# First loads in order of need on two queues, a constant zero for the warm-up products, and a new order of the first splits and products

## The chip, the cores and the metric

The kernel runs on one core of a Trainium2 chip. The metric is device time in microseconds (us), taken as the median of several executions. One further execution was recorded by the hardware profiler; every time inside the kernel below comes from that one.

The engines that matter here are PE (TensorE: matrix products into PSUM; its weight loads are shown as PEld), DVE (VectorE), ACT (ScalarE), POOL (GpSimd) and SP (SyncE, which issues most of the transfers). A q behind an engine's name means its sequencer, which issues transfers and handles semaphores.

## The reference

A gated mix of a Fourier mixing layer and a sliding-window attention, on one sequence of 2048 rows of 512 values, all in float32:

```python
x = A_x
g = sigmoid((x * gate_w).sum(-1, keepdims=True))
a = Cr @ (x @ Wr.T) - Ci @ (x @ Wi.T)          # real part of a two-dimensional DFT
q, k, v = split(x @ wqkv)                       # 32 heads of 16, window of 256
b = softmax(mask(q @ k.T / 4)) @ v @ wo
out = g * a + (1 - g) * b
```

## The kernel before

Precision is kept by splitting each float32 operand into a high part (rounded to PE's reduced float32 type, here called F32R) and a low part (what is left). A product of two such operands is three matrix products: high by high, high by low and low by high. The list of these pairs is `TERMS` (line 248); the first number picks the part of the weight `w`, or of `x` in the row projections, the second that of the other operand.

The whole program is one long stream of PE products with an order written by hand (manual schedules for PE, ACT, DVE and SP; POOL's order is left to a planner). The stages run into each other: projections of q, k and v, scores, softmax, attention, the two DFT stages and the output projection. A generator, `dense()` (line 595), yields the dense products, and the attention's work is put between them.

What matters here is how the stream begins, before the stages overlap:

- **Loads** (lines 147 to 159). `wraw` takes the weights of the first group of q and k, 128 x 1024, in four blocks of 256 columns, one for each quarter `dk` of the contraction. `XRAW[dk, 0]` takes the first 512 rows of x, transposed, as four blocks of 128 x 512. ACT's queue issues x blocks 0 and 1; SP's queue issues w block 0, w block 1, x blocks 2 and 3 in one transfer, and w blocks 2 and 3 in one transfer. Behind them SP issues the two halves of the v weights (`wv`, 512 KB each) and the next rows of x.
- **Splits** (lines 160 to 164). For each `dk`: ACT copies w to its high part (`wq0[0]`), x is split by `split_x` (high part by DVE for block 0 and by ACT for blocks 1 to 3, line 80 or 82; low part by DVE, line 85), and then DVE makes w's low part (line 164). Each engine works in this order.
- **Warm-up** (`warm()`, line 590). Eight products of a zero tile (128 x 128 weights, 512 columns, F32R) go to PE before anything else. The zero tile is cleared by DVE at line 151.
- **First products** (`qk_first()`, line 263). 24 products of 512 columns: for each `dk`, for each of the three terms, for q and for k. Each adds into one of two PSUM tiles.
- **What follows.** The v projections (`v_proj` through `row_proj`, line 304) take the same x and the split v weights `wvs` (`late(split_raw, r, True)`, line 601: high parts by ACT, low parts by DVE, behind the splits above on both engines).
- **POOL.** Line 203 fills the unused rows of one pad tile; its input `first_lo` is a piece of `wq0[1]`, read only to give it a place in the order. Eight memsets of the ring's spare rows (line 200) follow.

Tiles come from rotating pools: `pt` has four buffers (the first three hold `wraw` and x's first four blocks), and `ev` has five, one of them the zero tile.

The numbers that a transfer waits for are semaphores. The program has eight of them for transfers and hands them out in program order, so that a ninth transfer waits on its queue until the first has landed.

Of the kernel before, what the change touches and what calls it, by code (L numbers as in the profile page):

```python
# [7 lines left out]
F32 = mybir.dt.float32  # L8
F32R = mybir.dt.float32r
# [5 lines left out]
P = 128  # L15
# [4 lines left out]
NP = 4  # L20
# [6 lines left out]
WARM = 8  # L27
# [5 lines left out]
def fnet_window_mix(ctx: ExitStack, tc: tile.TileContext, xT, x, wqk, wv, wr, wi, cr, ci, wo, gw, out):  # L33
    nc = tc.nc
# [4 lines left out]
    ev = ctx.enter_context(tc.tile_pool(name="ev", bufs=5))  # L39
# [15 lines left out]
    def ld(dst, src):  # L55
        mark("sp", nc.sync.dma_start(dst, src))

    def f(ap):
        return ap.bitcast(F32)
# [4 lines left out]
    def mark(e, ins):  # L64
        last[e] = ins.ins
# [12 lines left out]
    def split(hi, lo, raw, act=False):  # L78
        if act:
            nc.scalar.copy(hi, raw)  # L80
        else:
            cast = (nc.gpsimd if act is None else nc.vector).tensor_copy(hi, raw)
            if act is None:
                mark("pool", cast)
        return nc.vector.tensor_sub(lo, raw, f(hi))
# [44 lines left out]
    XRAW = {}  # L130
# [7 lines left out]
    def split_x(ss, dks, act=False):  # L138
        for dk in dks:
            XT[dk, ss] = big.tile([P, 2, 512], F32R, name="big")  # L140
            mark("dve", split(XT[dk, ss][:, 0], XT[dk, ss][:, 1], XRAW.pop((dk, ss)), act))


    def pt_raw():
        return at.tile([P, NP, WIN], F32, name="pt", bufs=4).rearrange("p a b -> p (a b)")[:, :1024]

    with tc.manual_schedule(engines={mybir.EngineType.Activation, mybir.EngineType.DVE, mybir.EngineType.SP}):
        wraw, *xraw = [pt_raw() for _ in range(3)]
        wq0 = [st.tile([P, 1024], F32R, name=h) for h in ("hi", "lo")]
        zero = ev.tile([P, 512], F32R, name="ev")  # L150
        nc.vector.memset(f(zero[:]), 0.0)
        for dk in range(DK):
            XRAW[dk, 0] = xraw[dk // 2][:, HALVES[dk % 2]]
            if dk < 2:
                nc.scalar.dma_start(XRAW[dk, 0], xT[0, dk])
        for c in (slice(0, 256), slice(256, 512)):
            ld(wraw[:, c], wqk[0][:, c])
        ld(xraw[1].rearrange("p (k s) -> p k s", k=2), xT[0, 2:4].rearrange("k p s -> p k s"))
        ld(wraw[:, 512:], wqk[0][:, 512:])
        for dk in range(DK):  # L160
            c = slice(dk * 256, dk * 256 + 256)
            mark("act", nc.scalar.copy(wq0[0][:, c], wraw[:, c]))
            split_x(0, (dk,), dk > 0)
            mark("dve", nc.vector.tensor_sub(wq0[1][:, c], wraw[:, c], f(wq0[0][:, c])))


    NPAD = 2
# [31 lines left out]
        with behind("pool"):  # L199
            mark("pool", nc.gpsimd.memset(f(ring[i][96:128, :, ss * 512:(ss + 1) * 512]), 0.0))  # L200

    first_lo = f(wq0[1][96:128, 0:P]).unsqueeze(1).to_broadcast([32, NP, P])
    mark("pool", nc.gpsimd.affine_select(pads[0][0][96:128], first_lo, pattern=[[0, NP], [0, P]],
                                         compare_op=OP.is_gt, fill=0.0, base=0, channel_multiplier=0))
    for ss in range(4):
# [42 lines left out]
    TERMS = ((0, 0), (0, 1), (1, 0))  # L248
# [9 lines left out]
    def qk_evict(g, ss, i, ps):  # L258
        hl = hl_tile()
        split_psum(hl[:, 0], hl[:, 1], ps, -SCALE if i == 0 else 1.0)  # L260
        ld(qk_scr[i][g][ss].rearrange("h x s -> x h s"), f(hl[:]))

    def qk_first(w):
        pss = [ps_a.tile([P, 512], F32, name="s", tag="st") for _ in range(2)]
        for dk in range(DK):
            for n, (a, b) in enumerate(TERMS):
                for i in range(2):
                    c = dk * 256 + i * 128
                    nc.tensor.matmul(pss[i], w[a][:, c:c + 128], XT[dk, 0][:, b],  # L269
                                     start=dk == 0 and n == 0, stop=dk == 3 and n == 2)  # L270
        for i in range(2):
            qk_evict(0, 0, i, pss[i])
# [316 lines left out]

    def warm():  # L590
        ps = ps_d.tile([P, 512], F32, name="dv", tag="d")
        for i in range(WARM):
            nc.tensor.matmul(ps, zero[:, :128], zero, start=i == 0, stop=i == WARM - 1)  # L593

    def dense():
        warm()
        with behind("sp"):
            wraw = [load_raw(wv[i]) for i in range(2)]
            load_x(1, 0)
            load_x(1, 1)  # L600
        wvs = [late(split_raw, r, True) for r in wraw]
        qk_first(wq0)
        load_x(2, 0)
        load_x(2, 1)
# [416 lines left out]
    for n in range(N + LAG + 1):  # L1021
        k = n - LAG
# [90 lines left out]
```

## Time and profile before

| what | us |
|---|---|
| median of 3 runs | 845.59 |
| lowest and highest | 845.48 and 845.86 |
| the profiled execution, its own time | 845.1 |
| its span, first to last instruction | 843.3 |
| PE busy | 838.5 |
| PEld busy | 695.8 |
| DVE busy | 643.8 |
| ACT busy | 611.1 |
| POOL busy | 298.8 |

How to read the rows shown below: a row of the timeline has the start in us from the beginning of the span, the duration in us, the engine, the line of the kernel, the operation, the tile written and the tiles read, the shape, the number of instructions merged in the row, and in brackets how long the engine had been idle before and what released it. The duration of a merged row runs from the first start to the last end. Ends of products are modelled, so the distance between starts tells PE's pace. PEld rows are the weight loads that go ahead of each product. In the rows on transfers, q1 is SP's queue and q10 is ACT's.

### The profile page before, as it was taken

The page shows a single profiled execution, that of the slowest core. Times are in us where ns is not written, and L with a number is a line of the kernel's source. Part 1 is how long each engine was busy: PE and PEld are TensorE (multiplying, and loading weights), DVE is VectorE, ACT ScalarE, POOL GpSimd, SP SyncE. Part 2 cuts the span into 40 slices and gives each one's busy share as a digit, 9 for nine tenths or more (in the row PEclk, how much of TensorE's full clock was granted, in tenths as well). Part 3 has the DMA queues.
Part 4 walks back from the last instruction along what each step waited for, and adds up shares of the span by engine and source line. Part 5 has one row for each costly group of instructions (what it writes and reads, how often), then busy time and mean ns, then how long its engine had stood idle before and what let it go on. Part 6 is the DMA issues. An engine that isn't in the chain of part 4 may idle for free.

```text
span 843.3 us, 17171 instructions
## 1 busy us (share of the span) xinstructions
PE 838.5 (99%) x5310; PEld 695.8 (83%) x5310; DVE 643.8 (76%) x2083; ACT 611.1 (72%) x1832; POOL 298.8 (35%) x606
## 2 busy tenths in 40 slices
PE   9999999999999999999999999999999999999998
PEld 7888888888888888888888887878887878878997
DVE  5588978677979787787877877878987867666874
ACT  6488888878888897787877977867777865553430
POOL 8102333233232233342333243343242357756410
PEclk9999999999999999999999999999999999999999
DMA  8776678485766173534454547979874256455732
GB/s 295 251 227 187 217 243 283 159 259 202 220 222 189 54 232 107 177 120 121 140 160 126 168 153 223 298 214 309 274 216 149 96 179 198 137 192 196 220 133 92
DMA packets 94475, 161.03 MB, mean 191 GB/s; under 512 B 26800, under 2 KB 35504, under 8 KB 94384
## 3 DMA queue, kind: packets, MB, share of 16 engines
q1 hardware_dynamic: 93952, 159.28, 59.1%
q8 instruction: 42, 0.69, 0.3%
q10 hardware_dynamic: 432, 0.66, 0.2%
q14 instruction: 49, 0.40, 0.1%
HBM read 108.27 MB, written 51.64 MB: 190 GB/s over the span
## 4 chain that ended last, share of the span: by engine, by line
PE 99%; DVE 1%; issue 0%; ACT 0%; DVEq 0%; ACTq 0%
PE dc L529 42%; PE dab L304 11%; PE dqk L281 10%; PE t L449 9%; PE s L367 8%; PE o L475 8%; PE dv L304 5%; PE t L922 5%; PE s L269 1%; PE dv L593 0%; PE s L387 0%; DVE pad L350 0%; PE t L559 0%; DVE sm L369 0%; ACT sm L372 0%
## 5 line engine op out<-in xcount | busy, mean ns | idle before, releaser
L529 PE MATMUL dc<-big,hi 128*128 128x512 f32 x1020 | 344.7, 393 | 0.0
L369 DVE CUSTOM_DVE_ANT_0 sm<-s,mask 128x320 f32<-128x320 f32 (+4 forms) x512 | 235.5, 465 | 111.4 <-PE s L367 71.2
L372 ACT ACTIVATE sm<-sm,ml 128x320 f32<-128x320 f32 (+4 forms) x512 | 278.2, 544 | 56.4 <-DVE ml L369 52.1
L450 ACT ACTIVATE pt<-t 128x320 f32<-128x320 f32 (+4 forms) x392 | 159.5, 411 | 83.4 <-PE t L449 78.1
L529 PE MATMUL dc<-big,lo 128*128 128x512 f32 x510 | 200.2, 393 | 0.0
L529 PEld LDWEIGHTS dc<-big,hi 128*128 128x128 f32 x1020 | 179.3, 188 | 21.4
L454 POOL TENSOR_SCALAR_AFFINE_SELECT pt<-pt 128x128 f32<-128x128 f32 x196 | 77.1, 393 | 275.0 <-ACT pt L450 273.7
L449 PE MATMUL t<-ring,pad 128*128 128x320 f32 (+4 forms) x512 | 156.8, 306 | 0.0
L367 PE MATMUL s<-ring,pad 128*128 128x320 f32 (+4 forms) x512 | 154.9, 303 | 0.1
L350 DVE TENSOR_SCALAR pad<-ring,half 96x256 fp32r<-96x256 f32 x384 | 120.0, 359 | 5.4 <-PE t L449 4.9
L449 PEld LDWEIGHTS t<-ring,pad 128*128 128x128 f32 x512 | 96.1, 188 | 30.9 <-issue 8.7
L367 PEld LDWEIGHTS s<-ring,pad 128*128 128x128 f32 x512 | 96.2, 188 | 20.6 <-DVE ml L369 0.7
L529 PEld LDWEIGHTS dc<-big,lo 128*128 128x128 f32 x510 | 95.9, 188 | 12.0
L372 ACT ACTIVATION_READ_ACCUMULATOR sm<-sm,ml 128x1 f32 x512 | 98.1, 192 | 0.0
L588 DVE TENSOR_TENSOR lo<-raw,hi 128x512 fp32r<-128x512 f32 x137 | 94.3, 696 | 2.7 <-ACT hi L588 2.5
L304 PE MATMUL dab<-hi,big 128*128 128x512 f32 x256 | 88.9, 394 | 0.0
L281 PE MATMUL dqk<-big,hi 128*128 128x512 f32 x240 | 85.0, 393 | 0.0
L432 POOL TENSOR_SCALAR vpad<-vr,half 128x256 f32<-128x256 f32 x64 | 62.2, 983 | 62.1 <-PE o L475 29.5
L348 ACT ACTIVATE pad<-ring,half 96x256 fp32r<-96x256 f32 x128 | 66.9, 522 | 0.0
L454 POOL TENSOR_SCALAR_AFFINE_SELECT home<-home 128x128 f32<-128x128 f32 x60 | 33.8, 564 | 90.2 <-ACT home L450 85.7
L458 POOL TENSOR_SCALAR_AFFINE_SELECT pt<-pt 128x128 f32<-128x128 f32 x172 | 62.9, 366 | 0.0
L588 DVE CAST hi<-raw 128x512 fp32r<-128x512 f32 x126 | 54.3, 437 | 11.3 <-PE dc L529 10.6
(122 smaller groups left out, 1034.2 us busy)
## 6 DMA issues: line engine op xcount, KB each, us to landing
qk_scr<-home SPq DMA_DIRECT2D x32, 512.0 KB
ring<-qk_scr SPq DMA_DIRECT2D x32, 512.0 KB
raw<-cr SPq DMA_DIRECT2D x32, 512.0 KB
raw<-ci SPq DMA_DIRECT2D x32, 512.0 KB
r_scr<-ev SPq DMA_DIRECT2D x42, 256.0 KB
ab_scr<-home SPq DMA_DIRECT2D x20, 512.0 KB
big<-ab_scr SPq DMA_DIRECT2D x20, 512.0 KB
ring<-qk_scr SPq DMA_DIRECT2D x32, 256.0 KB
```

The lines of the kernel that those rows point to most:

```text
L281: nc.tensor.matmul(ps, w[a][:, c:c + 128], XT[dk, ss][:, b], start=n == 0, stop=n == 11)
L304: nc.tensor.matmul(ps, XT[dk, ss][:, a, c * 128:(c + 1) * 128], wh[b], start=n == 0, stop=n == 11)
L350: mark(f"pad{i}", nc.vector.tensor_scalar(dst, src, half[:96, h:h + 1], None, op0=OP.mult))
L367: nc.tensor.matmul(ps[:, :w], PAD[0, n][:, p], ring[1][:, p, k0:k0 + w], start=True, stop=True)
L369: mark("dve", nc.vector.tensor_tensor_reduce(out=sm[:, :w], in0=ps[:, :w], in1=mask[:, WIN - w:], scale=1.0, scalar=3e38, op0=OP.add, op1= ...
L372: mark("act", nc.scalar.activation(sm[:, :w], sm[:, :w], AF.Exp, bias=nm[:, c], scale=-1.0, accum_out=l[:, c]))
L449: nc.tensor.matmul(ps[:, :w], PAD[1, n][:, p], ring[0][:, p, q0:q0 + w], start=True, stop=True)
L450: nc.scalar.activation(pt[:, p, :w], ps[:, :w], AF.Exp, scale=-1.0)
L454: nc.gpsimd.affine_select(a, a, pattern=[[0, 2], [2, 64]], compare_op=OP.is_ge, fill=0.0, base=1, channel_multiplier=-1)
L475: nc.tensor.matmul(OT[g, sb][32 * p:32 * p + 32, q - sb * 512:e - sb * 512], v2[:, p], pt[:, p, q - q0:e - q0], start=first, stop=kb == 8 ...
L529: nc.tensor.matmul(ps, w[a][:, i % 8 * 128:i % 8 * 128 + 128], ab[SC[i]][:, b], start=i == ends[0] and a + b == 0, stop=i == ends[1] and a ...
L588: return fn(*args)
```

## The change

- The first transfers: x blocks 0 and 1 are each cut by partitions, 96 on ACT's queue and the other 32 on SP's. SP's order is now w block 0, the rest of x block 0, w block 1, the rest of x block 1, w blocks 2 and 3, x block 3. ACT's order is x block 0, x block 1 (96 partitions each), x block 2. There are nine transfers instead of six.
- The splits: block 0 of w gets its high part from DVE instead of ACT, and block 0 of x gets its high part from ACT instead of DVE. In each block DVE now makes w's low part ahead of x's.
- `qk_first` multiplies w's low part second and x's low part third.
- POOL's line 203 reads a piece of w's low part from block 1 instead of block 0.
- The warm-up products read a program-wide float32 constant, 128 x 128, instead of a cleared tile. They are 128 columns wide and in full float32 rather than F32R. The cleared tile and its memset are gone.

```diff
-        zero = ev.tile([P, 512], F32R, name="ev")
-        nc.vector.memset(f(zero[:]), 0.0)
         for dk in range(DK):
             XRAW[dk, 0] = xraw[dk // 2][:, HALVES[dk % 2]]
-            if dk < 2:
-                nc.scalar.dma_start(XRAW[dk, 0], xT[0, dk])
-        for c in (slice(0, 256), slice(256, 512)):
+        for dk in range(2):
+            c = slice(dk * 256, dk * 256 + 256)
+            nc.scalar.dma_start(XRAW[dk, 0][:96], xT[0, dk][:96])
             ld(wraw[:, c], wqk[0][:, c])
-        ld(xraw[1].rearrange("p (k s) -> p k s", k=2), xT[0, 2:4].rearrange("k p s -> p k s"))
+            ld(XRAW[dk, 0][96:], xT[0, dk][96:])
+        nc.scalar.dma_start(XRAW[2, 0], xT[0, 2])
         ld(wraw[:, 512:], wqk[0][:, 512:])
+        ld(XRAW[3, 0], xT[0, 3])
         for dk in range(DK):
             c = slice(dk * 256, dk * 256 + 256)
-            mark("act", nc.scalar.copy(wq0[0][:, c], wraw[:, c]))
-            split_x(0, (dk,), dk > 0)
-            mark("dve", nc.vector.tensor_sub(wq0[1][:, c], wraw[:, c], f(wq0[0][:, c])))
+            if dk:
+                mark("act", nc.scalar.copy(wq0[0][:, c], wraw[:, c]))
+            else:
+                nc.vector.tensor_copy(wq0[0][:, c], wraw[:, c])
+            nc.vector.tensor_sub(wq0[1][:, c], wraw[:, c], f(wq0[0][:, c]))
+            split_x(0, (dk,), True)
...
-    first_lo = f(wq0[1][96:128, 0:P]).unsqueeze(1).to_broadcast([32, NP, P])
+    first_lo = f(wq0[1][96:128, 256:256 + P]).unsqueeze(1).to_broadcast([32, NP, P])
...
-            for n, (a, b) in enumerate(TERMS):
+            for n, (a, b) in enumerate(((0, 0), (1, 0), (0, 1))):
...
+        zero = nc.const_aps.tensor(0.0, (P, 128), F32)
         for i in range(WARM):
-            nc.tensor.matmul(ps, zero[:, :128], zero, start=i == 0, stop=i == WARM - 1)
+            nc.tensor.matmul(ps[:, :128], zero, zero, start=i == 0, stop=i == WARM - 1)
```

## The prediction

> **What bounds the kernel now.** I read the page first: busy times, then the chain that ended last.
>
> ```profile
> span 843.3 us, 17171 instructions
> PE 838.5 (99%) x5310; PEld 695.8 (83%) x5310; DVE 643.8 (76%) x2083; ACT 611.1 (72%) x1832; POOL 298.8 (35%) x606
> PE 99%; DVE 1%; issue 0%; ACT 0%; DVEq 0%; ACTq 0%
> ```
>
> The program is one stream on PE. PE's order is fixed, so what the first products lose or gain moves nearly all that follows. The chain in order of time shows its head:
>
> ```profile
> 1.51 3.70 PE dv L593 x8
> 5.21 6.42 PE s L269 x24
> 11.62 10.88 PE dv L304 x48
> ```
>
> Eight warm-up products, 24 first products, then v. The 48 v products wait for nothing, so an unhindered product costs 10.88/48 = 0.227 us. PE's timeline gives the exact starts, and its weight loads show where it stood still:
>
> ```profile
> 4.66 0.55 PE L593 MATMUL dv<-ev 128*128 128x512 f32 x1
> 5.05 1.21 PE L269 MATMUL s<-big,hi 128*128 128x512 f32 x4
> 11.46 0.39 PE L304 MATMUL dv<-hi,big 128*128 128x512 f32 x1
> 4.85 0.38 PEld L269 LDWEIGHTS s<-big,hi 128*128 128x128 f32 x2 [0.28 <-issue]
> 5.52 0.30 PEld L269 LDWEIGHTS s<-big,hi 128*128 128x128 f32 x2 [0.28 <-DVE big L85]
> 7.17 0.30 PEld L269 LDWEIGHTS s<-big,hi 128*128 128x128 f32 x2 [0.42 <-DVE big L85]
> 8.33 0.30 PEld L269 LDWEIGHTS s<-big,hi 128*128 128x128 f32 x2 [0.41 <-ACT big L80]
> 9.06 0.30 PEld L269 LDWEIGHTS s<-big,hi 128*128 128x128 f32 x2 [0.43 <-DVE big L85]
> ```
>
> From 5.05 to 11.46 are 6.41 us for 24 products that need 24 x 0.227 = 5.44. So 0.97 us are stalls: three for x's low part (line 85), one for its high part (line 80). More than about 1 us can't be won here unless the first product starts earlier. What feeds PE:
>
> ```profile
> 0.97 0.48 DVE L151 MEMSET ev<- 128x512 f32 x1 [0.97 <-PEq L1105]
> 4.31 0.43 DVE L82 CAST big<-pt 128x512 fp32r<-128x512 f32 x1 [1.14 <-DMA pt<-xT]
> 5.38 0.42 DVE L164 TENSOR_TENSOR lo<-pt,hi 128x256 fp32r<-128x256 f32 x1
> 6.00 1.11 DVE L85 TENSOR_TENSOR big<-pt,big 128x512 fp32r<-128x512 f32 x1 [0.20 <-ACT big L80]
> 8.31 0.69 DVE L85 TENSOR_TENSOR big<-pt,big 128x512 fp32r<-128x512 f32 x1 [0.86 <-ACT big L80]
> 10.32 2.49 DVE L85 TENSOR_TENSOR lo<-raw,hi 128x512 fp32r<-128x512 f32 x4
> 4.04 0.41 ACT L162 CAST hi<-pt 128x256 fp32r<-128x256 f32 x1 [1.04 <-DMA pt<-wqk]
> 5.34 0.62 ACT L80 CAST big<-pt 128x512 fp32r<-128x512 f32 x1
> 7.35 0.41 ACT L162 CAST hi<-pt 128x256 fp32r<-128x256 f32 x1 [1.39 <-DMA pt<-wqk]
> 9.02 2.19 ACT L80 CAST hi<-raw 128x512 fp32r<-128x512 f32 x4
> ```
>
> w block 0 lands at 4.04, x block 0 at 4.31, w blocks 2 and 3 at 7.35. The last is late because 512 KB of x stand ahead of it on SP's queue.
>
> **The loads.** Moved bytes from the span's start to 3.6, 4.25, 6.0 and 6.5 us:
>
> ```profile
> q10 hardware_dynamic: 128, 0.24, 17.9%
> q1 hardware_dynamic: 182, 0.17, 16.2%
> DMA packets 499, 0.68 MB, mean 159 GB/s; under 512 B 42, under 2 KB 296, under 8 KB 499
> DMA packets 876, 1.37 MB, mean 229 GB/s; under 512 B 77, under 2 KB 333, under 8 KB 876
> DMA packets 971, 1.57 MB, mean 241 GB/s; under 512 B 87, under 2 KB 343, under 8 KB 971
> ```
>
> x block 0 is 0.26 MB on q10 (ACT), all moved at about 3.7 us with 0.45 MB moved in total, and told 0.6 to 0.7 us later. After the change blocks 0 of w and x are 0.39 MB on both queues. If w's last bytes and x block 1's first ones mix in as the shares of the two rows say, some 0.43 MB have moved when the last of x block 0 has. That is at most 0.06 MB less, and the rate is 0.4 MB/us (0.69 MB from 4.25 to 6.0). So x block 0 lands between 4.16 and 4.31; I take 4.31, since 0.43 is near 0.45, and w block 0 stays at 4.04, first on its queue.
>
> Later blocks gain. w block 1 and x block 1 are complete at 0.69 and 0.82 MB, at about 4.3 and 4.6. w blocks 2 and 3 landed 0.85 us after their last byte (1.05 MB of q1 and 0.52 of q10 make 1.57, at 6.5, told at 7.35); with this longer delay they land by 5.1 and 5.5. All of block 2 is moved at 1.31 MB, 5.85, and lands at 6.7, 0.65 earlier than now. x block 3 is last, at 1.57 MB: 7.35.
>
> Three more transfers are issued, and SP has a new wait:
>
> ```profile
> 2.17 0.47 SPq L56 DMA_DIRECT2D pt<-wqk  x1
> 4.30 0.38 SPq L56 DMA_DIRECT2D pt<-xT  x1
> ```
>
> Before, the ninth transfer in program order, the next rows of x, went out at 4.30, when the first had landed. After, x block 3 is the ninth: it waits until about 4.1, and both halves of wv queue behind it, out by 5.2 instead of 3.7. q1 is busy with the blocks before until 5.85, so this costs nothing; without that backlog, x block 3 would land at the earliest 2.6 us after its issue (1.2 to the first byte as at the start, 0.65 to move, 0.7 to be told), 6.9, still inside 7.35. wv keeps its place in the byte count and lands as before.
>
> **The splits.** x block 0's high part costs 0.62 on ACT instead of 0.43 on DVE. It is ready at 4.31 + 0.62 = 4.93 instead of 4.74, and the first product, 0.2 behind its weight load, starts at 5.18 instead of 5.05: 0.13 lost (bounds: 0.02 gained, if x lands at 4.16, to 0.19 lost). w block 0's high part on DVE has this row of another tile as its price:
>
> ```profile
> L82 DVE CAST ring<-tw 128x256 fp32r<-128x256 f32 x6 | 1.7, 310 | 0.0
> ```
>
> That is 4.04 to 4.35, its low part to 4.8, both hidden by ACT's cast of x.
>
> From 5.18, with 1.36 us a block, PE asks for each block's high parts at 5.18, 6.54, 7.90 and 9.26, for w's low part 0.45 later and for x's 0.91 later. ACT (0.41 and 0.62 a block): x block 1 ready at 6.14, block 2 from 6.7 to 7.75, block 3 to 8.8. All in time, block 2 by 0.15 only. DVE (0.42 and 0.69): x block 0 low at 5.7 (asked at 6.09), block 1 at 6.9, or 7.3 if POOL's line 203, which now starts with w block 1's low part near 6.1, stretches this subtraction to 1.11 as it does now (asked at 7.45); block 2 at 8.5 (8.81), block 3 at 9.5 (10.17). The new order of terms buys these margins: under the old one x's low part would be asked for 0.45 earlier, and blocks 0 to 2 would be late by a tenth or more. So the 0.97 us go.
>
> Next to be late would be v. ACT's four casts of wv begin at 8.8 instead of 9.02, and DVE's four subtractions at about 9.75 instead of 10.32, so they end at 10.4, 11.05, 11.65 and 12.25. PE then starts v at 5.18 + 5.44 = 10.62 and asks for them at 10.85, 11.53, 12.21 and 12.9. No stall.
>
> **The warm-up.** The memset (0.48) falls away, off the path; PE need not wait for it and can begin near 0.9 (between 0.79, when the first transfers are issued, and 1.51). A product of 128 columns in full float32 stands elsewhere in the trace:
>
> ```profile
> L475 PE MATMUL o<-pt,vpad 128*32 128x320 f32 x400 | 31.4, 436 | 0.0
> 118.45 0.72 PE L475 MATMUL o<-pt,vpad 128*32 128x320 f32 x8
> 118.72 0.72 PE L475 MATMUL o<-pt,vpad 128*32 128x320 f32 x8
> ```
>
> 400 records there and 112 on another tile make 512, twice the 256 products of 320 columns that the loops make, and four side by side take 118.72 - 118.45 = 0.27 us. So a float32 product is two passes of 0.27/320 us a column: 128 columns cost 0.216, about what 512 F32R columns cost (0.227). The old warm-up ran at half of that pace:
>
> ```profile
> 2.10 1.05 PE L593 MATMUL dv<-ev 128*128 128x512 f32 x2
> ```
>
> From 2.10 to 4.66 are six products, 0.427 each. The new ones take the same 3.4 us and end near 4.5. The full pace began between 4.66 and 5.05, 3.15 to 3.54 after PE's start; the profile's clock row is 1.00 throughout and doesn't show it. Counted from 0.9 it comes by 4.44, at the same instant as before by 5.05, both ahead of 5.18. Cost nothing, with the warm-up as cover.
>
> **Sum.** -0.97 + 0.13 = -0.84 us. The profiled execution, 845.1 (843.3 and 1.8 around it), becomes 844.3. It lies 0.5 below the median of 845.59, so I predict 845.59 - 0.84 = 844.8. Its own range: block 2 late by another 0.4 gives 845.2; x at 4.16 gives 844.6; 0.2 of scatter each way makes 844.4 to 845.4.
>
> **Rivals.** *The pace falls back* (slower). PE idles from 4.5 to 5.18, as it doesn't now. If the full pace isn't granted or isn't kept over that gap, the first products run at 0.427 until PE has been busy for another 3.54 us: 8.3 slow products and 15.7 fast ones, 7.1 us, v at 12.28 instead of 11.46: 0.8 slower, 846.4. It decides once more than four products run slow (4 x 0.2 = 0.8). If all 24 do, v starts at 15.43, 4 us late: 849.6. For it: the gap is new. Against: by any count the busy stretch is as long as the old one. The Trainium skill (TensorE: Matmul & The Clock Gate, "What's actually happening") says that the window is about 3.4 us long and free-running, not started by the kernel; by that rule a window that ends inside the new gap's reach could miss and the loss above follows. The 3.15 to 3.54 us here agree with its length, and no run here shows its phase.
>
> *The stall only moves*: block 2 or wv lands later than counted and half of the 0.97 comes back, 845.2 to 845.6. For it: 0.15 us of margin on block 2. Against: x block 3 and wv each have 0.4 or more.
>
> *Later waits fall differently.* PE's weight loads wait for nothing shown in the profile here:
>
> ```profile
> PEld t L449 <- issue: 8.7, 20, 0.5
> PEld o L475 <- issue: 5.3, 15, 0.4
> ```
>
> A shifted start can drop or add some; five of 0.4 are 2 us: 842.8 or 846.8. Against: the same waits came in every run, within 845.48 to 845.86.
>
> **How the numbers follow.** Forecast 0.56; stall moves 0.12; pace falls back for a window 0.08, for the whole block 0.06; later waits 0.18, of which 0.12 beyond 0.2% faster and 0.06 beyond 0.2% slower. 0.2%, 1.7 us, is about what a measurement of this kernel can tell from no change. So faster 0.12, slower 0.12, within 0.76. The range runs from 843.5, which takes in half of the faster case, to 846.8, past the pace rival.
>
> **What would show it.** Right: line 269's first start at 5.0 to 5.2, 24 products with starts 0.227 apart, v from 10.5 to 10.8, no idle before the weight loads put down to line 85. Wrong: starts 0.427 apart in line 269, warm-up products far from 0.43 each, a wait for w blocks 2 and 3 past 6.9, or v's weight loads waiting for line 85. The forecast fails outright if PE's first product starts after 5.6 or v before 10.2.

## The result and the profile after

The changed kernel takes 849.56 us (848.87 to 850.43, median of 6 runs), the kernel before 845.54 in the runs beside it. The ratio is 1.0051, with a 95% interval from 1.0038 to 1.0063: slower by half a per cent, where 844.8 was forecast and 846.8 was the upper end of the range. The profiled execution took 850.43, the slowest of the six, and its span is 848.5, 5.2 more than before.

The page of the changed kernel, span, busy times and the shares of the chain that ended last:

```profile
span 848.5 us, 17195 instructions
PE 840.9 (99%) x5318; PEld 698.2 (82%) x5318; DVE 644.2 (76%) x2082; ACT 610.1 (72%) x1832; POOL 298.0 (35%) x606
PE 96%; DVE 1%; DMA 1%; ACT 0%; issue 0%; SPq 0%; DVEq 0%; ACTq 0%
```

PE's share of the chain falls from 99% to 96%, and two transfers have entered it: one at its head, and a store near 111 us, which is most of the 1%. The rows of the chain (start, duration, what; ... stands for rows left out):

```profile
0.80 0.39 SPq L56
1.19 0.06 issue
1.24 3.44 DMA pt<-xT
...
4.76 1.28 ACT L80
6.04 0.01 issue
6.05 0.63 ACT big L80
6.68 0.04 issue
6.72 7.37 PE s L272 x24
14.09 10.88 PE dv L307 x48
...
111.11 7.50 DMA qk_scr<-home
```

Before, the chain began with the warm-up. Now it begins with SP's second transfer, the 32 partitions of x block 0, then 1.28 us of ACT, then the cast of x, then PE. The timeline of ACT names the 1.28 us, first in the kernel before and then in the changed one:

```profile
1.71 1.28 ACT L162 ACT_TABLE_LOAD   x1 [1.71 <-PEq L1105]
```

```profile
4.76 1.28 ACT L80 ACT_TABLE_LOAD   x1 [4.76 <-DMA pt<-xT]
6.05 0.62 ACT L80 CAST big<-pt 128x512 fp32r<-128x512 f32 x1
6.58 0.40 ACT L163 CAST hi<-pt 128x256 fp32r<-128x256 f32 x1
```

Ahead of ACT's first operation the compiler puts a load of ACT's function table. In the kernel before, it ran at 1.71 while ACT waited for data anyway. In the changed one it starts only when a piece of x block 0 has landed, and stands in full between x and its cast. PE's timeline:

```profile
0.83 3.75 PE L597 MATMUL dv<-const-float32-0.0 128*128 128x128 f32 x16 [0.83 <-PEq L1109]
6.72 1.22 PE L272 MATMUL s<-big,hi 128*128 128x512 f32 x2 [2.14 <-ACT big L80]
7.75 1.05 PE L272 MATMUL s<-big,lo 128*128 128x512 f32 x2
8.60 1.86 PE L272 MATMUL s<-big,hi 128*128 128x512 f32 x4
10.29 0.63 PE L272 MATMUL s<-big,lo 128*128 128x512 f32 x2
13.93 0.39 PE L307 MATMUL dv<-hi,big 128*128 128x512 f32 x1
```

PE stands idle for 2.14 us. From 7.75 to 10.29 are six products, 0.42 each: half pace; the two ahead of them take 0.59 and 0.43. The sixteen from 10.29 to 13.93 take 0.23 each. So v starts at 13.93 instead of 11.46, 2.47 late:

- The first product starts 1.67 late: x block 0 lands at 4.76 instead of 4.31 (+0.45), table load (+1.28), cast on ACT instead of DVE (+0.19), and 0.25 less between the cast and the product.
- The 24 products take 7.21 instead of 6.41. Eight slow ones cost 1.77 over the 5.44 of an unhindered set, and the 0.97 of stalls are gone.

That is half of the 5.2. PE stays 2.47 late up to 68 us. The next loss shows in DVE's timeline, before and after:

```profile
67.54 1.66 DVE L350 TENSOR_SCALAR pad<-ring,half 96x256 fp32r<-96x256 f32 x2
69.12 0.68 DVE L90 TENSOR_TENSOR home<-dqk,home 128x512 fp32r<-128x512 f32 x1
```

```profile
70.01 2.78 DVE L353 TENSOR_SCALAR pad<-ring,half 96x256 fp32r<-96x256 f32 x2
72.71 0.68 DVE L90 TENSOR_TENSOR home<-dqk,home 128x512 fp32r<-128x512 f32 x1
```

The first row is 2.47 later, the second 3.59: two small DVE instructions have taken 1.12 longer, and PE's next v product needs what line 90 writes. Its weight load before and after, with the wait in brackets:

```profile
69.85 0.19 PEld L304 LDWEIGHTS dv<-hi,big 128*128 128x128 f32 x1 [0.15 <-DVE home L90]
```

```profile
73.44 0.19 PEld L307 LDWEIGHTS dv<-hi,big 128*128 128x128 f32 x1 [1.27 <-DVE home L90]
```

POOL's timeline over the same stretch, before and after:

```profile
66.48 1.18 POOL L588 CAST hi<-raw 128x512 fp32r<-128x512 f32 x2 [28.79 <-PE dqk L281]
67.63 2.73 POOL L588 TENSOR_TENSOR lo<-raw,hi 128x512 fp32r<-128x512 f32 x2
```

```profile
68.89 1.18 POOL L591 CAST hi<-raw 128x512 fp32r<-128x512 f32 x2 [28.74 <-PE dqk L284]
70.04 2.60 POOL L591 TENSOR_TENSOR lo<-raw,hi 128x512 fp32r<-128x512 f32 x2
```

POOL casts and subtracts the next group's weights (`split_soon`). It is 2.41 later than before where DVE is 2.47 later, so POOL is 0.06 ahead, and its first subtraction now begins 0.03 behind DVE's start (70.04 against 70.01) instead of 0.09 (67.63 against 67.54). Before, DVE's first pad instruction was done in 0.34 and only the second (1.39) met a subtraction; now both do (1.48 and 1.38, overlapping a little).

Two further steps, at 90 to 95 us (about 0.55) and at 115 to 118 us (about 0.7), and 0.2 near 285 complete the loss. The one near 115 is a wait of ACT for the store of the chain above (before, after):

```profile
113.67 0.60 ACT L88 ACTIVATE home<-dab 128x512 fp32r<-128x512 f32 x1 [0.75 <-DMA qk_scr<-home]
```

```profile
118.70 0.60 ACT L88 ACTIVATE home<-dab 128x512 fp32r<-128x512 f32 x1 [1.67 <-DMA qk_scr<-home]
```

### The profile page after: what moved, and what is told of

Its sections match the earlier page's. It is cut to its first block, busy times and chain, and to the rows that moved or that the text cites. A ratio compares the mean times of both kernels' runs of the same rounds, so it can differ in the third digit from the quotient of the medians.

```text
span 848.5 us, 17195 instructions
## 1 busy us (share of the span) xinstructions
PE 840.9 (99%) x5318; PEld 698.2 (82%) x5318; DVE 644.2 (76%) x2082; ACT 610.1 (72%) x1832; POOL 298.0 (35%) x606
## 4 chain that ended last, share of the span: by engine, by line
PE 96%; DVE 1%; DMA 1%; ACT 0%; issue 0%; SPq 0%; DVEq 0%; ACTq 0%
PE dc L532 42%; PE dab L307 10%; PE t L452 9%; PE dqk L284 9%; PE s L370 8%; PE o L478 8%; PE dv L307 5%; PE t L926 5%; DMA qk_scr<-home 1%; PE s L272 1%; DVE pad L353 1%; DMA pt<-xT 0%; DVE sm L372 0%; PE s L390 0%; PE t L562 0%
```

## The experiments

The questions: which part of the change makes x late, why the table load waits, what the idle stretch of PE costs, and what sets off the collision at 70 us. "Slow" counts line 269's products (272 after) at half pace, from their starts in PE's timeline; "pads" is the duration of the two DVE instructions above. One profiled execution each; the intervals are against runs of the kernel before on the same chip (medians 845.44 to 845.63).

| kernel | table load | cast of x block 0 | first product | slow | v | pads | median | ratio, interval |
|---|---|---|---|---|---|---|---|---|
| before | 1.71 | 4.31 | 5.05 | 0 | 11.46 | 1.66 | 845.54 | |
| after | 4.76 | 6.05 | 6.72 | 8 | 13.93 | 2.78 | 849.56 | 1.0051, 1.0038 to 1.0063 |
| x block 0 whole | 2.20 | 4.42 | 5.09 | 0 | 11.12 | 2.78 | 846.96 | 1.0023, 1.0014 to 1.0032 |
| early table | 2.19 | 4.74 | 5.42 | 0 | 11.97 | 2.78 | 848.22 | 1.0035, 1.0022 to 1.0048 |
| longer warm-up | 4.94 | 6.23 | 6.90 | 0 | 12.52 | 2.78 | 847.90 | 1.0027, 1.0015 to 1.0038 |
| new warm-up only | 1.72 | 4.38 | 4.96 | 0 | 11.50 | 1.66 | 846.10 | 1.0009, 1.0000 to 1.0017 |
| x blocks 0, 1 whole | 2.21 | 4.47 | 5.14 | 0 | 10.75 | 2.78 | 846.24 | 1.0014, 1.0005 to 1.0023 |
| the same, last block's old order | 2.20 | 4.47 | 5.14 | 0 | 10.79 | 1.66 | 845.33 | 0.9998, 0.9989 to 1.0006 |
| before, last block's new order | 1.72 | 4.29 | 5.09 | 5 | 11.98 | 2.78 | 846.29 | 1.0011, 1.0002 to 1.0019 |
| before, new orders only | 1.71 | 4.44 | 5.09 | 4 | 11.69 | 2.78 | 846.40 | 1.0009, 1.0000 to 1.0018 |
| before, new loads only | 2.20 | 4.90 | 5.47 | 2 | 12.28 | 1.66 | 846.52 | 1.0012, 1.0003 to 1.0021 |
| before, 18 warm-up products | 1.71 | 4.24 | 7.95 | 0 | 13.40 | 1.66 | 847.19 | 1.0019, 1.0010 to 1.0028 |

### x block 0 whole

The changed kernel with x block 0 in one transfer on ACT's queue; block 1 stays cut.

```diff
-            nc.scalar.dma_start(XRAW[dk, 0][:96], xT[0, dk][:96])
+            h = 96 if dk else 128
+            nc.scalar.dma_start(XRAW[dk, 0][:h], xT[0, dk][:h])
             ld(wraw[:, c], wqk[0][:, c])
-            ld(XRAW[dk, 0][96:], xT[0, dk][96:])
+            if dk:
+                ld(XRAW[dk, 0][96:], xT[0, dk][96:])
```

> The changed kernel, but x block 0 comes in one transfer on ACT's queue; all else as changed. Theory (the table load waits for x because ACT's first cast has two transfers to wait for, and PE goes slow in the idle time): with one transfer the table load carries no wait and runs near 2.2 us, x lands at 4.3 to 4.8, the first product starts at 5.2 to 5.7 instead of 6.72, all 24 first products start 0.227 apart, v starts at 10.7 to 11.2 instead of 13.93, total 844.7 to 846 against 849.6. Rival (the new warm-up alone is too short or too early, whatever the table load does): the first products still start 0.427 apart, v at 12.3 or later, total 846.5 or more.

Measured 846.96: 2.6 less than the changed kernel. ACT's timeline of this kernel:

```profile
2.20 1.28 ACT L80 ACT_TABLE_LOAD   x1 [2.20 <-issue]
4.42 0.62 ACT L80 CAST big<-pt 128x512 fp32r<-128x512 f32 x1 [0.94 <-DMA pt<-xT]
```

ACT's first operation is the same cast, but it has one transfer to wait for, and the table load runs at 2.20, right behind ACT's own DMA issues. In the program of the changed kernel the cast has two transfers to wait for, and one of the two waits stands on the table load ahead of it; in the kernel before and here the load carries none. No product is slow, v is at 11.12. So the head came as expected, but the total lies above the range expected (844.7 to 846): PE is 0.34 ahead of the kernel before at 68 us and 0.77 behind at 72. The profiled execution is the fastest of the twelve (845.86 to 850.33), so slow products in the others are not excluded.

### Table loaded early

The changed kernel, with ACT copying one column of a constant right after the DMA issues.

```diff
         ld(XRAW[3, 0], xT[0, 3])
+        scrap = const.tile([P, 1], F32, name="scrap")
+        nc.scalar.copy(scrap, nc.const_aps.tensor(1.0, (P, 1), F32))
```

> The changed kernel with one thing added: ACT copies one constant column behind its transfers, so that the table load has nothing to wait for; x block 0 stays in two transfers. Theory: table load near 2.2, x lands at about 4.75 as in the changed kernel, first product at 5.5 to 5.7, starts 0.227 apart, v at 11.0 to 11.2, total 845 to 846. Rival (the split transfers or the exchange of the casts cost the time, not the table load): first product at 6.5 or later, total above 848.

Measured 848.22, 1.3 less. ACT's timeline:

```profile
2.19 1.28 ACT L161 ACT_TABLE_LOAD   x1 [2.19 <-issue]
4.74 0.62 ACT L80 CAST big<-pt 128x512 fp32r<-128x512 f32 x1 [1.07 <-DMA pt<-xT]
```

The load goes to 2.19, the cast starts when x has landed, at 4.74, and the first product at 5.42, 1.30 earlier: the price of the load. The gap of PE shrinks to 0.83 and no product is slow in the profiled execution, v is 1.96 earlier. What is left against the whole block is x's own lateness: block 0 lands 0.3 later, and PE stands for 0.49 before block 1. v (11.97) and the total missed the theory, which left this out, and the total is the rival's (above 848): the table load is a part of the loss, not all of it. PE is 0.51 behind the kernel before at v, 1.6 after the pads and 2.7 at 118 us.

### A longer warm-up

```diff
-WARM = 8
+WARM = 19
```

> The changed kernel with 19 warm-up products instead of 8, which should keep PE busy until near 6.7; the table load still waits. Theory: first product still at 6.7 to 6.9, but all 24 start 0.227 apart, v at 12.1 to 12.4 instead of 13.93, total 1.5 to 2 us below the changed kernel, 847.6 to 848.1. Rival (the eight slow products come from the new kind of warm-up product, which does not open the full pace): they stay 0.427 apart, total 849 or more.

Measured 847.90, 1.7 less, though the first product starts no earlier (6.90). PE is busy to the end of the wait, and its 24 products all run at full pace: v at 12.52 instead of 13.93, 1.41 earlier, and the new kind of product does open the full pace. This is the price of the slow products when the wait itself is left as it is. That the idle stretch made them slow is likely but not shown: two kernels below have four and five slow products with no gap ahead of them.

### The new warm-up alone

The kernel before with the constant zero for the warm-up.

```diff
-        zero = ev.tile([P, 512], F32R, name="ev")
-        nc.vector.memset(f(zero[:]), 0.0)
...
+        zero = nc.const_aps.tensor(0.0, (P, 128), F32)
         for i in range(WARM):
-            nc.tensor.matmul(ps, zero[:, :128], zero, start=i == 0, stop=i == WARM - 1)
+            nc.tensor.matmul(ps[:, :128], zero, zero, start=i == 0, stop=i == WARM - 1)
```

> The kernel before with the new warm-up alone (constant zero, 128 columns, float32, no memset). Theory: warm-up from 0.83 to 4.4, first product at 5.05 as before after an idle 0.5 us, full pace, v at 11.46, total 845.5 within 0.4. Rival (an idle gap of half a us, or the kind of product, is enough to lose the full pace): starts 0.427 apart, v at 12.2 or later, total 846.3 or more.

Measured 846.10, 0.2 above the range expected, and within 0.1% of before (interval 1.0000 to 1.0017). PE idles from 4.58 to 4.96 and goes on at full pace; v is at 11.50. So at the head the warm-up costs nothing in this execution, the fastest of the eleven; by the medians it is 0.5 slower, which the interval does not set clear of no change. In the profile PE falls from 0.17 behind at 115 us to 0.60 behind at 117.

### Whole blocks 0 and 1, and the collision put on and taken off

First, the changed kernel with both blocks whole on ACT's queue.

```diff
-            nc.scalar.dma_start(XRAW[dk, 0][:96], xT[0, dk][:96])
+            nc.scalar.dma_start(XRAW[dk, 0], xT[0, dk])
             ld(wraw[:, c], wqk[0][:, c])
-            ld(XRAW[dk, 0][96:], xT[0, dk][96:])
```

> The changed kernel with x blocks 0 and 1 each in one transfer of 128 partitions on ACT's queue; order of the transfers, exchange of casts, order of splits and terms and the warm-up as changed. Theory (cutting x by partitions 96 and 32 lowers the rate of the transfers from 0.40 to about 0.28 MB/us, and gives ACT's first cast a second wait): from 3.6 to 5 us the rate is 0.38 or more, the table load runs near 2.2, x block 1's cast on ACT starts before 5.8, first product at 5.0 to 5.2, v at 10.5 to 10.9 instead of 13.93. POOL's first cast of the second group's weights still has three waits, so the loss of 1.1 us near 70 us stays; total 845.3 to 846.5. Rival (the rate falls because nine transfers are in flight on two queues, not because of the cut): rate 0.31 or less, x block 1 at 6 us or later, v at 11.1 or later.

Measured 846.24, 3.3 less than the changed kernel: the cut is most of the loss. The 24 products take 5.61 (5.14 to 10.75), almost the 5.44 of an unhindered set, and v is 0.71 ahead of the kernel before. At 70 us the pads take 2.78, and the lead becomes a lag of 0.41.

Since POOL's order of instructions is the same in all these kernels, I looked at what POOL's first cast at 66 us waits for. In the kernel before it has four waits (DVE, a transfer, PE, ACT), in the changed one three: with x's low part as DVE's last split the wait for ACT is dropped. With PE's shift taken off, the cast starts at 66.482 with four waits (five of the twelve kernels) and at 66.425 with three (the other seven), and "pads" is 1.66 in the five and 2.78 in the seven. Two kernels test that alone. The one above with the old order of DVE in the last of the four blocks:

```diff
-            nc.vector.tensor_sub(wq0[1][:, c], wraw[:, c], f(wq0[0][:, c]))
+            if dk < 3:
+                nc.vector.tensor_sub(wq0[1][:, c], wraw[:, c], f(wq0[0][:, c]))
             split_x(0, (dk,), True)
+            if dk == 3:
+                nc.vector.tensor_sub(wq0[1][:, c], wraw[:, c], f(wq0[0][:, c]))
```

> As e5_whole_blocks, and in the last block alone DVE makes x's low part ahead of w's, as in the kernel before. That gives POOL's first cast of the second group's weights its fourth wait (on ACT) back. Theory: the head as in e5_whole_blocks (v at 10.5 to 10.9), POOL's cast 0.058 us later against PE than in the changed kernel, DVE's two pad instructions near 70 us take 1.7 us together instead of 2.8, no loss there; total 844.3 to 845.3, below both kernels. Rival (the loss near 70 us comes from the earlier or later start as such): it is there again, total as e5_whole_blocks.

And the kernel before with the new order in the last block:

```diff
+            if dk == 3:
+                nc.vector.tensor_sub(wq0[1][:, c], wraw[:, c], f(wq0[0][:, c]))
             split_x(0, (dk,), dk > 0)
-            mark("dve", nc.vector.tensor_sub(wq0[1][:, c], wraw[:, c], f(wq0[0][:, c])))
+            if dk < 3:
+                nc.vector.tensor_sub(wq0[1][:, c], wraw[:, c], f(wq0[0][:, c]))
```

> The kernel before with one thing changed: in the last block DVE makes w's low part ahead of x's. POOL's cast then has three waits instead of four. Theory: the head as before within 0.4 us (x's low part of block 3 is 0.42 later), POOL's cast 0.058 us earlier against PE, DVE's pad instructions near 68 us take 2.8 us instead of 1.7, PE loses 1.0 to 1.1 us there; total 846.3 to 847.2 against 845.6. Rival: no loss near 70 us, total 845.4 to 846.0.

DVE's timeline of the first of the two, then of the second, and POOL's of the second:

```profile
66.89 1.66 DVE L355 TENSOR_SCALAR pad<-ring,half 96x256 fp32r<-96x256 f32 x2
```

```profile
68.06 2.78 DVE L353 TENSOR_SCALAR pad<-ring,half 96x256 fp32r<-96x256 f32 x2
```

```profile
66.94 1.18 POOL L591 CAST hi<-raw 128x512 fp32r<-128x512 f32 x2 [28.46 <-PE dqk L284]
68.08 2.60 POOL L591 TENSOR_TENSOR lo<-raw,hi 128x512 fp32r<-128x512 f32 x2
```

Two instructions at 10 us exchanged on DVE take the collision at 68 us away or bring it: 845.33 against 846.24, and 846.29 against the kernel before. The first pair's intervals just touch (0.9989 to 1.0006, 1.0005 to 1.0023). In the profiles PE loses 1.1 there or nothing (0.52 late becomes 1.63 in the second; 0.66 ahead stays so in the first). The second also had five slow first products, though its first product started at 5.09 without a gap; the last section comes back to this.

845.33 is the best of all, with no difference from before that can be told (0.9989 to 1.0006). It starts v 0.67 earlier than the kernel before and is 0.24 behind it at 117 us: 0.2 goes near 94 us and 0.70 near 115, at ACT's wait for the store. SP's queue before and in this kernel:

```profile
103.88 1.02 SPq L56 DMA_DIRECT2D raw<-x  x2
104.99 0.38 SPq L56 DMA_DIRECT2D qk_scr<-home  x1
```

```profile
103.45 2.81 SPq L56 DMA_DIRECT2D raw<-x  x2
106.37 0.38 SPq L56 DMA_DIRECT2D qk_scr<-home  x1
```

The two loads are issued in 2.81 instead of 1.02 (the first alone in 2.34 instead of 0.54), so the store behind them goes out 1.4 later, and ACT's wait for its landing grows, as in the profile after. What holds the load could not be read from the traces; it was held in some kernels with the collision and some without. But it was held (2.16 to 3.01 for the two) in six of the seven kernels with the new warm-up, the one with nothing else new among them, and in none of the five with the old (1.02 to 1.25); the seventh, with 19 products, has 1.02. These are single executions, and nothing tests it by itself: it stays open.

### The orders alone

The kernel before with the new order of terms, w's low part first in blocks 1 to 3, and POOL's new piece.

```diff
+            if dk:
+                nc.vector.tensor_sub(wq0[1][:, c], wraw[:, c], f(wq0[0][:, c]))
             split_x(0, (dk,), dk > 0)
-            mark("dve", nc.vector.tensor_sub(wq0[1][:, c], wraw[:, c], f(wq0[0][:, c])))
+            if not dk:
+                nc.vector.tensor_sub(wq0[1][:, c], wraw[:, c], f(wq0[0][:, c]))
...
-            for n, (a, b) in enumerate(TERMS):
+            for n, (a, b) in enumerate(((0, 0), (1, 0), (0, 1))):
```

> The kernel before with the new order of terms in the first products, the new order on DVE in blocks 1 to 3 and the new input of POOL's line 203; loads, casts and warm-up as before. Theory: first product at 5.05, three of the four stalls shrink, the one for w blocks 2 and 3 (landing at 7.35) stays, v at 10.9 to 11.2 instead of 11.46; the loss of 1.1 near 70 us appears (three waits); total 845.9 to 846.6. Rival (the order of terms alone brings the whole gain and nothing is lost later): total 845.0 or less.

Measured 846.40. Four slow products (0.8 us) hide what the order may gain: the 24 take 6.60, and v, at 11.69, is later than expected. The collision is there and costs 1.12.

### The loads alone, and a late start alone

The kernel before with the nine new first transfers:

```diff
-            if dk < 2:
-                nc.scalar.dma_start(XRAW[dk, 0], xT[0, dk])
-        for c in (slice(0, 256), slice(256, 512)):
+        for dk in range(2):
+            c = slice(dk * 256, dk * 256 + 256)
+            nc.scalar.dma_start(XRAW[dk, 0][:96], xT[0, dk][:96])
             ld(wraw[:, c], wqk[0][:, c])
-        ld(xraw[1].rearrange("p (k s) -> p k s", k=2), xT[0, 2:4].rearrange("k p s -> p k s"))
+            ld(XRAW[dk, 0][96:], xT[0, dk][96:])
+        nc.scalar.dma_start(XRAW[2, 0], xT[0, 2])
         ld(wraw[:, 512:], wqk[0][:, 512:])
+        ld(XRAW[3, 0], xT[0, 3])
```

> The kernel before, with the changed kernel's nine first transfers and nothing else of the change; ACT's first operation then still has one transfer to wait for. Theory (the cut by partitions itself makes x late; the table load is late only where ACT's first operation waits for two transfers): table load near 2 us; x block 0 on DVE at 4.6 to 4.8, first product 5.3 to 5.5 instead of 5.05, x blocks 1 to 3 late too, v at 11.9 to 12.6 instead of 11.46; the last block's order on DVE is the old one, so no collision of POOL and DVE near 70 us; time 846.0 to 846.8. Rival, my prediction's count (transfers at 0.4 MB/us, x block 0 by 4.31, w blocks 2 and 3 earlier by 0.65): first product at 5.05, v at 11.2 to 11.5, time 845.3 to 845.6.

Measured 846.52, in the theory's range, with x block 0 0.1 later than it had. x block 0 is late although nothing but the loads has changed, and the table load, with one wait behind it (w block 0), is not. The windows of 3.6 to 5.0 and 5.0 to 6.5 us show the rate, in the last column in GB/s: before, after, and this kernel.

```profile
3.60:5.00 1.40, 1.40 (x4) 0.92 (x4) 0.65 (x2) 0.48 (x2) 0.00 (x0) 1.00 1.07 405
5.00:6.50 1.50, 1.50 (x7) 1.09 (x7) 1.30 (x3) 0.95 (x2) 0.56 (x1) 1.00 1.04 389
```

```profile
3.60:5.00 1.40, 0.98 (x5) 0.68 (x4) 0.72 (x2) 0.24 (x1) 0.00 (x0) 1.00 1.07 277
5.00:6.50 1.50, 0.00 (x0) 0.00 (x0) 0.00 (x0) 1.49 (x2) 0.00 (x0) 1.00 1.07 308
```

```profile
3.60:5.00 1.40, 1.40 (x4) 0.77 (x3) 0.10 (x1) 0.41 (x1) 0.00 (x0) 1.00 1.02 260
5.00:6.50 1.50, 1.31 (x4) 0.83 (x4) 1.35 (x3) 0.00 (x0) 0.00 (x0) 1.00 1.07 324
```

The 16 DMA engines count as busy all the time in each (the column before it), but with the cut they move 17 to 36% less. With both blocks whole the same windows give 377 and 411, and with only block 1 cut 311 and 343, so it is the cut and not the order of the transfers. Each cut block also adds a transfer (seven, eight, nine); whether the shape of the pieces or their number does it is not separated. The rate is not the only harm: w block 1 stands behind the rest of x block 0 on SP's queue, and ACT gets it at 6.61 here, 4.92 before.

The kernel before with `WARM = 18`, a later start and nothing else:

> The kernel before with 18 warm-up products instead of 8: a later start of the first products and nothing else. Theory (what PE loses at the start is carried to the end, and the further 1.1 us near 70 us come from POOL's wait count, not from the lateness): warm-up until about 7.3, first product 7.3, 24 products at 0.227 without stalls, v at 12.7 to 12.8 (+1.3), two pad instructions of DVE near 68 us in 1.7 and no loss there, end +1.3 to +2.0, time 846.8 to 847.6. Rival 1 (a late start runs by itself into further waits): pads in 2.8, end +2.4 or more, time 848 or more. Rival 2 (later slack takes the lateness up): end +0.5 or less, time 846.1 or less.

Measured 847.19, 1.6 more. The start is later than expected (7.95, since eleven warm-up products and not eight ran at about half pace), v at 13.40, 1.94 late. The pads take 1.66, PE is 1.93 late at 68 and at 95 us, 2.2 at 125 us and 1.9 at the end. So a late start is carried to the end, and does not by itself bring the collision.

## Why the prediction was wrong

The step that failed is "ready at 4.31 + 0.62 = 4.93 … the first product … starts at 5.18 instead of 5.05". It started at 6.72, past the 5.6 at which the prediction said that it would fail.

- **The table load** was not in the sum at all. Its row stood in the timeline of ACT at 1.71, free there, and I quoted ACT's casts without it. The change moves ACT's first operation to a tile filled by two transfers, and the load then takes on one of the waits: 1.28 on the path, shown by the early copy (1.30 earlier) and by the whole block (load at 2.20).
- **The loads.** "the rate is 0.4 MB/us": 405 GB/s before, but 277 after, since the cut itself lowers it. x block 0 landed at 4.76 where I took 4.31, outside both of my bounds. "w block 1 and x block 1 … land by 5.1 and 5.5": w block 1 came at 6.61 with the loads alone. I moved bytes about in a rate taken from uncut transfers.
- **The warm-up.** Length and end were right (16 records, 0.213 apart, the last from 4.16, so an end near 4.4; the modelled end is 4.58). "Cost nothing, with the warm-up as cover" was wrong: the gap I counted as 0.7 was 2.14. The rival *the pace falls back* names the mechanism and its size: 8.3 slow products priced, 8 seen, and the longer warm-up takes them away. Whether the full pace was never granted or was lost in the gap can't be read from the trace. The rival carried 0.14, on a gap three times too short. That its price for 24 slow products, 849.6, is also the measured time is chance.
- **The stalls.** "So the 0.97 us go" holds: with whole blocks the 24 products take 5.61 where 5.44 were counted, and no stall of line 85 is left. *The stall only moves* did not come. With x in time the head gains 0.71, close to the 0.84 forecast.
- **What follows.** "What the first products lose or gain moves nearly all that follows" is right for a pure delay (18 warm-up products: 1.94 at v, 1.9 at the end). It was no reason to stop the sum at v: the order of two DVE instructions changed POOL's waits and cost 1.1 near 70 us. I followed line 164 to PE and line 203, not to the next instruction of POOL that waits for DVE. *Later waits fall differently* allowed for such a loss, but with no place.

By the runs the loss divides so: the cut with all that hangs on it (x late, table load, slow products) 3.3 (849.56 to 846.24), the collision 0.9 (846.24 to 845.33); the gain at the head, 0.7, is given back near 94 us (0.2) and near 115 us (0.7), for a reason left open. The parts inside the 3.3 overlap: the early table alone is worth 1.3, the longer warm-up alone 1.7. The profile's sum to v, 2.47, and its 5.2 in all are of the slowest execution; the medians differ by 4.0, and how many products were slow in the others isn't known.

## What to carry to other kernels

Look up the first operation of ACT and count the transfers that it waits for: one operation on a tile from a single source, early, keeps the table load off the path. Before cutting a transfer to make it land earlier, measure the rate of cut transfers, not of whole ones. After reordering an engine's instructions, follow the semaphores to engines that wait for its last one; in a tuned kernel 0.06 us can decide a collision worth a microsecond.

## What the runs showed of the hardware

**The pace of PE starts at its own time.** The warm-up of the kernel before starts at 1.51 in every kernel that has it, but the full pace begins at different times: by 5.05 before, at 7.2 with the last block's new order (five slow products), by 6.3 with 18 warm-up products. PE's timelines of the latter two:

```profile
1.51 3.78 PE L596 MATMUL dv<-ev 128*128 128x512 f32 x8 [1.51 <-DVE ev L151]
5.09 1.91 PE L272 MATMUL s<-big,hi 128*128 128x512 f32 x4
6.79 0.80 PE L272 MATMUL s<-big,lo 128*128 128x512 f32 x2
```

```profile
1.51 6.60 PE L593 MATMUL dv<-ev 128*128 128x512 f32 x18 [1.51 <-DVE ev L151]
```

In the first, four products take 6.79 - 5.09 = 1.70, 0.43 each, without any gap ahead of them. In the second, 18 products take 7.95 - 1.51 = 6.44: by their starts the first takes 0.59, nine take 0.43, one 0.39 and seven 0.23. So up to 3.5, 5.7 and 4.8 us of busy PE were needed. The new warm-up starts at 0.83, and its records drop from 0.213 to 0.112 by 3.73 with 19 products and by 3.87 with both blocks whole and the last block's old order, after 2.9 and 3.0 us. The profile's clock row shows 1.00 in all of them. The Trainium skill (TensorE: Matmul & The Clock Gate, "What's actually happening") has a window of about 3.4 us that runs free of the kernel's start. That the time varies agrees with it; the 2.9 and 3.0 here are less than one such window, and 5.7 is 1.7 of them. So the slow products of one profiled execution say little of the next, and the medians decide.

**A collision of DVE and POOL costs the whole instruction.** One pad instruction takes 0.34 where it starts 0.09 ahead of POOL's subtraction, and 1.38 to 1.48 where it meets one; nothing in the waits shows it, only the duration. The Trainium skill (SBUF — State Buffer, "SBUF: two separate sides") describes a lock on a pair of ports that DVE and GpSimd share, held for a whole instruction; one subtraction takes 1.30 to 1.43, which agrees. The profile doesn't show the ports, and by its rows the pad instruction that is held in the changed kernel starts 0.03 ahead of the subtraction.

**Where a semaphore wait stands has a price.** POOL's cast started 0.058 later with four waits than with three. The traces show what differs: with four, the wait for PE, the last to be met, stands on a separate instruction of POOL's sequencer, which ends at 66.40 in the kernel before, and the cast starts 0.08 behind it; with three, the cast carries that wait itself.
